# Decode attention: the first softmax ahead of a key turn, five value steps ahead of the second group's scores, and wq loaded in two parts

## Chip, cores, metric

One core of a Trainium2 chip. The metric is device time in microseconds (us), median over executions. Before the change: 326.44 us over three runs when the prediction was made (325.81 to 326.68). Repeats on one chip spread by 0.3 to 2%, and chips differ a little. A program on one core has no second die to compare with. In some groups 1 to 3 runs are marked slow, because they lie over 1.5% above the fastest run of the same kernel; the ratios leave these out, the medians include them.

## The reference

Two transformer layers that share weights and caches, one token for each of four sequences ("batches" below):

```python
x = x + attn(layernorm(x))     # wq, K and V caches, softmax, wo
x = x + ffn(layernorm(x))      # gelu(x@w_gate) * (x@w_up) @ w_down
x = x + attn(layernorm(x))     # the same weights, the same caches
x = x + ffn(layernorm(x))
# B=4, D=512, Hq=32, Hkv=8, Sk=4096, Dh=128, F=1792, bfloat16
```

The caches are 32 MB of keys and 32 MB of values. The kernel reads the keys once (they stay in SBUF for the second layer) and the values nearly twice.

## The kernel before

For each batch, 8 key heads are handled as two groups of 4. A key head is two tiles of 16 x 128; each tile is turned on VectorE (DVE) with a 32 x 32 block transpose, in place: a "key turn", 16 per batch. TensorE multiplies turned keys with queries into one PSUM bank per group (`scores`), DVE and ScalarE do the softmax, and TensorE multiplies the probabilities with the values in 16 "value steps" per batch, one step for each 0.5 MB unit. Values stream through a ring of 7 such slots. A load is issued from the SyncE queue as soon as the program order and a free slot allow.

The order of everything is the order of the program text; no scheduler moves anything. The part that the change touches, for one batch:

```python
        sc1 = new_scores(0)
        scores(sc1, ga, 0)
        turn(1 if first else GH)          # key turns 1 to 8 end here
        if two:
            vals2.step(...)               # second layer of the batch before
        scores(sc1, ga, 1)
        turn()                            # turn 9, a key of the second group
        p0 = soft(sc1)                    # max, exp ... of the first group
        turn()                            # 10
        ...
        soft_turn(p0)
        pe, den = soft_swap(p0, p1p), soft_den(p0)
        turn()                            # 11
        prob1[ga] = (pe, soft_recip(den))
        ...
        build_q1(b1, gb)
        turn()                            # 12
        vals.step(2)                      # value steps 1 and 2
        turn(3)                           # 13 to 15
        sc1 = new_scores(0)
        scores(sc1, gb, 0)                # needs turns 9, 11, 13 and 15
        turn()                            # 16
        vals.step(3)                      # 3 to 5
        scores(sc1, gb, 1)
        ...
        p0 = soft(sc1)
        vals.step(3)                      # 6 to 8
        ...
        vals.step(3)                      # 9 ..., need the second group's softmax
```

A value step, cut to what matters. After steps 4, 8 and 12 a copy on DVE takes two heads' sums out of PSUM (after steps 14 and 16 one head's); it is called the OT copy below:

```python
        def step(self, count=1):
            for _ in range(min(count, VB - self.n)):
                ...
                self.n += 1
                load_v()
                v = slot(held[b, g, s, t])
                for i in range(CH):
                    nc.tensor.matmul(self.ot[:, s % 2], lhsT=v[:, i, :], rhs=pe[:, s, c, :], ...)
                release(held.pop((b, g, s, t)))      # the slot is free
                load_v()                             # issue what now fits
                if self.n % (m * NT) == 0:           # m * NT is 4 (2 in the last four steps)
                    nc.vector.tensor_tensor(out=self.dst(...), in0=self.ot[...],
                                            in1=rden[...], op=ALU.mult)     # the OT copy
```

Of the kernel before, what the change touches and what calls it, by code (L numbers as in the profile page):

```python
# [9 lines left out]
BF16 = mybir.dt.bfloat16  # L10
# [5 lines left out]
P = 128  # L16
# [3 lines left out]
QD = 4  # L20
QS = P // QD
# [9 lines left out]
def kernel(  # L31
# [15 lines left out]
    _, Hkv, Sk, Dh = A_k_cache.shape  # L47
    HqDh = A_wq.shape[1]
    Hq = HqDh // Dh
    rep = Hq // Hkv  # L50
    F = B_w_gate.shape[1]
    assert Sq == 1 and Dh == P and rep == QD and Hkv % GH == 0
    KD = D // P
# [4 lines left out]
    NG = Hkv // GH  # L58
    HG = GH * rep
    NK = GH * BE  # L60
    W = 4 * QD
    TG = GH * NT
# [3 lines left out]
    wts = ctx.enter_context(tc.tile_pool(name="wts", bufs=1))  # L66
# [15 lines left out]

    dq = nc.sync

    wq_sb = wts.tile([P, KD, HqDh], BF16, name="wq_sb")
    wo_sb = wts.tile([P, Hq, D], BF16, name="wo_sb")
    wg_sb = wts.tile([P, KD, F], BF16, name="wg_sb")
    wu_sb = wts.tile([P, KD, F], BF16, name="wu_sb")
# [3 lines left out]
    wq_dram = A_wq.rearrange("(k p) n -> p k n", p=P)  # L92
# [22 lines left out]
    def groups(b):  # L115
        return [b % NG, (b + 1) % NG]
# [1 line left out]
    def cache_tile(cache, b, kvh, t, n=1):  # L118
        return cache[b, kvh].rearrange("(p c) d -> p c d", p=P)[:, t * CH:(t + n) * CH]

    def load_wq():
        dq.dma_start(out=wq_sb[:], in_=wq_dram)

    def load_rest():
        n = Hq // 4
# [84 lines left out]
    def new_rows():  # L210
        turn_row[0] += 1
        return ROWS[turn_row[0] % 2]
# [5 lines left out]
    def q_rows(b0, nb, g):  # L218
        bs = slice(b0, b0 + nb)
        rows = new_rows()  # L220
        for k in range(KD):
            for j in range(QD):
                n0 = (g * QD + j) * rep * Dh
                w = wq_sb[:, k, n0:n0 + rep * Dh].rearrange("p (m i e) -> p m e i", i=QS, e=2)
                nc.tensor.matmul(rows[j * QS:j * QS + nb, :], lhsT=xn_bf[:, k, bs], rhs=w,  # L225
                                 start=(k == 0), stop=(k == KD - 1))
        return rows
# [16 lines left out]
    def q_build(qm, g):  # L244
        qe = ps_sm.tile([P, NK, rep], FP32, name="qe", tag="sm")
        nc.tensor.matmul(qe[:], lhsT=t32_bf.rearrange("p a i -> p (a i)"),  # L246
                         rhs=qm.rearrange("p g n h -> p (g n) h"), start=True, stop=True)
        dst = qb[:, W:].rearrange("p (n x a h) -> p n x a h", x=2, a=QD, h=rep)[:, :, 0]
        nc.vector.tensor_tensor(  # L249
            out=dst,  # L250
            in0=qe[:].unsqueeze(2).broadcast_to([P, NK, QD, rep]),
            in1=amask[:].unsqueeze(1).unsqueeze(3).broadcast_to([P, NK, QD, rep]),
            op=ALU.mult)
# [98 lines left out]
    class Keys:  # L352
# [19 lines left out]
        def turn(self, count=1):  # L372
            for _ in range(count):
                kvh, t = self.tile(self.nt)
                self.nt += 1
                words = KT[kvh][t].rearrange("p c d -> p (c d)").bitcast(FP32)
                nc.vector.transpose(out=words, in_=words)  # L377

    def new_scores(bank):
        return ps_sc.tile([P, CH, QS], FP32, name="sc", tag=f"sc{bank}")  # L380

    def scores(sc, g, t):
        for be in range(BE):
            for s in range(GH):
                n = s * BE + be
                w0 = n * 2 * W + (W if t == 0 else 0)
                kt = KT[g * GH + s][t].rearrange("p c (b j e) -> p c b j e", b=NB, e=2)
                nc.tensor.matmul(sc[s * QS:(s + 1) * QS], lhsT=qb[:, w0:w0 + 2 * W],  # L388
                                 rhs=kt[:, :, be // 2, :, be % 2],
                                 start=(t == 0 and be == 0), stop=(t == NT - 1 and be == BE - 1))  # L390
# [22 lines left out]
    def soft_turn(p0):  # L413
        flat = p0[0].rearrange("p c j -> p (c j)")
        nc.vector.transpose(out=flat, in_=flat)  # L415

    def soft_den(p0):
        zx = p0[1]
        den = ps_sm.tile([P, GH, rep], FP32, name="den", tag="sm")
        nc.tensor.matmul(den[:], lhsT=mean_f[:, :], rhs=zx[:], start=True, stop=True)  # L420
        return den
# [26 lines left out]
    for b in range(B - 1):  # L448
        n = early[b]
# [72 lines left out]
    def attend(b2, b1, next_q=None, rest=None):  # L522
        two, first = b2 is not None, b1 == 0
        prob1, prob2 = {}, {}
        ga, gb = groups(b1)
        keys = Keys(b1)
        turn = keys.turn
        vals = Values(b1, 0, prob1, lambda k, m: OT_bf[:, k * rep:(k + m) * rep])
        vals2 = None
        if two:  # L530
            vals2 = Values(b2, 1, prob2, lambda k, m: OT2_bf[:, k * rep:(k + m) * rep, b2])
            sc2 = [new_scores(i) for i in range(NG)]
            seen["hold"] = True
            scores(sc2[0], ga, 0)
            keys.load(GH)
            qm1 = next_q()
            scores(sc2[0], ga, 1)
            keys.load(GH)
            q_build(qm1, gb)
            rest(1)  # L540
            for t in range(NT):
                scores(sc2[1], gb, t)
            if early[b2] < TG:
                keys.load(TG)
                seen["hold"], seen["whole"] = False, True
                load_v()
            else:
                keys.load(GH)
            p0 = soft(sc2[0])
            rest(1)  # L550
            soft_turn(p0)
            pe0, den0 = soft_swap(p0, p2p), soft_den(p0)
            rest(VB)
            qm = q_spread(q1_bf[:, ga, :, b1], amask, ga)
            turn()
            prob2[ga] = (pe0, soft_recip(den0))
            q_build(qm, ga)
            turn(3)
            vals2.step(2 * NT)
            if early[b2] == TG:  # L560
                keys.load(GH)
                seen["hold"], seen["whole"] = False, True
                load_v()
        else:
            load_wq()
            keys.load(2 * TG)
            load_v()
            make_identity(nc, ident_bf[:])
            build_consts()
            xT_ps = ps_sm.tile([P, KD, B], BF16, name="xT_ps", tag="sm")  # L570
            for k in range(KD):
                nc.tensor.transpose(xT_ps[:, k, :], x_bf[:B, k * P:(k + 1) * P], ident_bf[:B, :B])
            nc.vector.tensor_copy(out=XX[:, 0].rearrange("p b k -> p k b"), in_=xT_ps[:])
            ln_square(0, B)
            rstd1 = ln_rstd(B, ln_center(0, B))
            q_first(q_rows(0, B, 0), 0, rstd1)
            build_q1(0, 0)
            turn(TG - 1)
        sc1 = new_scores(0)
        scores(sc1, ga, 0)  # L580
        turn(1 if first else GH)
        if two:
            vals2.step(max(early[b2] - vals2.n - 1, 0))
        scores(sc1, ga, 1)
        turn()
        p0 = soft(sc1)
        turn()
        if two:
            vals2.step(early[b2] - vals2.n)
        soft_turn(p0)  # L590
        pe, den = soft_swap(p0, p1p), soft_den(p0)
        turn()
        prob1[ga] = (pe, soft_recip(den))
        if first:
            q_first(q_rows(0, B, 1), 1, rstd1)
        build_q1(b1, gb)
        turn()
        vals.step(2)
        turn(3)
        sc1 = new_scores(0)  # L600
        scores(sc1, gb, 0)
        turn()
        vals.step(3)
        scores(sc1, gb, 1)
        rows = new_rows()
        hp = 2 * rep
        heads = pairs(vals.order)
        p0 = soft(sc1)
        vals.step(3)
        soft_turn(p0)  # L610
        if not first:
            for i in range(2):
                out_proj(rows, OT_bf, heads[i], hp, i == 0)
        pe, den = soft_swap(p0, p1p), soft_den(p0)
        if two:
            p1 = soft(sc2[1])
        prob1[gb] = (pe, soft_recip(den))
        vals.step(3)
        if two:
            soft_turn(p1)  # L620
            pe1, den1 = soft_swap(p1, p2p), soft_den(p1)
            prob2[gb] = (pe1, soft_recip(den1))
        if first:
            vals.step(5)
            load_rest()
            seen["upto"] = len(loads)
            load_v()
            for i in range(3):
                out_proj(rows, OT_bf, heads[i], hp, i == 0, i == 2)
            y = y_select(y_rows(rows, 1), 1)  # L630
            return (y, OT_bf, heads[3], hp), vals2
        vals.step(2)
        out_proj(rows, OT_bf, heads[2], hp)
        vals.step()
        out_proj(rows, OT_bf, heads[4], rep, False, True)
        yc = y_rows(rows, 1)
        vals.step()
        y = y_select(yc, 1)
        vals.step()
        return (y, OT_bf, heads[5], rep), vals2  # L640
# [64 lines left out]
    for b in range(B):  # L705
# [17 lines left out]
        def next_q():  # L723
            return q_spread(turn_rows(q_rows(b, 1, gb), 512)[:, :, 0], am, gb)
# [46 lines left out]
```

## Time and profile before

| | before |
|---|---|
| median | 326.44 us |
| profiled execution, span | 327.2 us |
| bytes from HBM | 113.5 MB |
| DMA engines busy with the kernel's queue | 89.6% |
| TensorE, VectorE, ScalarE busy | 65%, 52%, 9% |

The page of the kernel before: the mean busy share of the 16 DMA engines and the GB/s in 40 equal slices of 8.2 us, the chain of waits by engine, and the group of key turns (count, then busy us and mean ns of one, then idle time ahead of it).

```profile
DMA  7999959999939998899989977999999999999910
GB/s 275 430 420 422 412 207 398 346 377 383 345 106 363 422 423 361 314 365 417 366 307 351 425 290 253 400 372 393 381 411 424 420 400 381 352 374 408 414 40 3
...
DMA 40%; PE 28%; DVE 19%; SPq 8%; issue 3%; ACT 1%; DVEq 0%; ACTq 0%
...
L377 DVE STREAM_TRANSPOSE kt<-kt 128x1024 f32<-128x1024 f32 x64 | 75.0, 1216 | 5.1 <-DMA kt<-in_A_k_cache_dram 5.1
```

Where nothing stalls, the DMA engines move about 420 GB/s and 1 MB takes 2.5 us. The largest share of the chain is DMA. So this kernel loses time where the DMA row falls: slices 6, 12, 16, 17, 21, 24 and 25, and the end.

Finer, the stretches in which the first-layer attention of each batch lets the DMA engines run dry (columns: stretch, length, busy us of TensorE, its weight loads, VectorE, ScalarE, GpSimd, then granted TensorE clock, DMA share, GB/s). The last line is the same place in the fourth batch:

```profile
40.00:44.00 4.00, 1.58 (x13) 0.56 (x13) 4.00 (x4) 0.00 (x0) 0.00 (x0) 0.50 0.70 280
44.00:48.00 4.00, 4.00 (x73) 1.81 (x65) 0.24 (x2) 0.00 (x0) 0.00 (x0) 0.50 0.34 101
...
128.00:132.00 4.00, 3.71 (x69) 2.10 (x72) 1.53 (x3) 0.00 (x0) 0.00 (x0) 0.50 0.69 219
...
192.00:196.00 4.00, 1.87 (x14) 0.56 (x13) 3.79 (x4) 0.00 (x0) 0.00 (x0) 0.50 0.65 266
196.00:200.00 4.00, 4.00 (x79) 2.10 (x75) 0.34 (x2) 0.00 (x0) 0.00 (x0) 0.50 0.44 145
...
272.00:276.00 4.00, 2.52 (x44) 1.05 (x42) 1.10 (x4) 0.00 (x0) 0.00 (x0) 0.50 0.99 406
```

In the first three batches the ring is full there, and value steps 3 to 5, which would free slots, stand in TensorE's queue behind the second group's scores, which wait for key turns. In the fourth batch there is no such hole (0.99).

The same place in the fourth batch in order of time on VectorE (start, length, engine, line, operation; in brackets the idle time before it and what ended it). The line at 254.60 is key turns 12 to 16:

```profile
248.10 1.25 DVE L377 STREAM_TRANSPOSE kt<-kt 128x1024 f32<-128x1024 f32 x1 [1.03 <-DMA kt<-in_A_k_cache_dram]
249.27 0.65 DVE L394 TENSOR_REDUCE m<-sc 128x1 f32<-128x512 f32 x1
...
254.60 5.74 DVE L377 STREAM_TRANSPOSE kt<-kt 128x1024 f32<-128x1024 f32 x5
262.12 0.17 DVE L513 TENSOR_TENSOR OT_bf<-ot,rden 128x8 bf16<-128x8 f32 x1 [1.78 <-PE ot L505]
264.38 0.69 DVE L394 TENSOR_REDUCE m<-sc 128x1 f32<-128x512 f32 x1 [2.10 <-PE sc L388]
```

And on TensorE:

```profile
254.04 0.58 PE L505 MATMUL ot<-pe,ring 128*128 128x4 bf16 x16
256.87 0.59 PE L505 MATMUL ot<-pe,ring 128*128 128x4 bf16 x16 [2.24 <-DMA ring<-in_A_v_cache_dram]
...
259.27 1.87 PE L388 MATMUL sc<-kt,qb 128*32 128x512 bf16 x13 [1.27 <-DVE kt L377]
261.07 1.44 PE L505 MATMUL ot<-pe,ring 128*128 128x4 bf16 x48
```

Step 1 runs at 254.04 without a wait, step 2 at 256.87 after waiting for a value load, the second group's scores follow their turns, and steps 3 to 5 come at 261.07 without any wait.

### The profile page before, as it was taken

What the parts mean: (1) busy time and instruction counts of PE and PEld (TensorE: products, weight loads), DVE (VectorE), ACT (ScalarE), POOL (GpSimd) and SP (SyncE); (2) the same over time, 40 slices, a digit from 0 to 9 for tenths busy, and PEclk for the clock granted to TensorE, in tenths of its full rate; (3) what the DMA queues carried; (4) which work ended last, traced back from release to release, by engine and by line L of the source; (5) the groups of instructions that cost most, each with busy time, mean ns of one, the idle gap of its engine ahead of it and who ended that gap; (6) DMA issues with size and microseconds to landing.
All of it is one profiled execution on the core that took longest, in us unless ns stands there. A gap on an engine that the chain in (4) does not pass through costs nothing.

```text
span 327.2 us, 8603 instructions
## 1 busy us (share of the span) xinstructions
PE 211.0 (65%) x3844; PEld 121.5 (37%) x3844; DVE 170.9 (52%) x481; ACT 29.1 (9%) x70; POOL 0.7 (0%) x6
## 2 busy tenths in 40 slices
PE   1224575243676346978876359799874597998875
PEld 0001344121323122555433125456331265654655
DVE  5097752013348657525457884254498752545133
ACT  0002002000002020300020102100101030002200
POOL 0000000000000000000000000000000000000000
PEclk9999555555558555555595555556765555559555
DMA  7999959999939998899989977999999999999910
GB/s 275 430 420 422 412 207 398 346 377 383 345 106 363 422 423 361 314 365 417 366 307 351 425 290 253 400 372 393 381 411 424 420 400 381 352 374 408 414 40 3
DMA packets 26789, 114.07 MB, mean 349 GB/s; under 512 B 2296, under 2 KB 8192, under 8 KB 18944
## 3 DMA queue, kind: packets, MB, share of 16 engines
q1 hardware_dynamic: 26752, 113.53, 89.6%
q8 instruction: 30, 0.49, 0.6%
q14 instruction: 7, 0.06, 0.0%
HBM read 113.51 MB, written 0.00 MB: 347 GB/s over the span
## 4 chain that ended last, share of the span: by engine, by line
DMA 40%; PE 28%; DVE 19%; SPq 8%; issue 3%; ACT 1%; DVEq 0%; ACTq 0%
DMA kt<-in_A_k_cache_dram 20%; DMA ring<-in_A_v_cache_dram 17%; PE sc L388 8%; DVE kt L377 7%; PE ot L505 7%; PE rows L314 3%; DMA wd_sb<-in_B_w_down_dram 3%; SPq L127 3%; SPq L133 3%; PE y L347 2%; DVE rows L215 2%; PE rows L280 2%; PE rows L225 2%; PE x L434 1%; DVE pp L415 1%
## 5 line engine op out<-in xcount | busy, mean ns | idle before, releaser
L388 PE MATMUL sc<-kt,qb 128*32 128x512 bf16 x512 | 63.7, 547 | 26.6 <-DVE kt L377 22.4
L505 PEld LDWEIGHTS <-ring 128*128 128x128 bf16 x1920 | 59.5, 105 | 51.3 <-DMA ring<-in_A_v_cache_dram 28.3
L377 DVE STREAM_TRANSPOSE kt<-kt 128x1024 f32<-128x1024 f32 x64 | 75.0, 1216 | 5.1 <-DMA kt<-in_A_k_cache_dram 5.1
L505 PE MATMUL ot<-pe,ring 128*128 128x4 bf16 x1920 | 62.1, 166 | 21.8 <-DMA ring<-in_A_v_cache_dram 20.7
L215 DVE STREAM_TRANSPOSE rows<-rows 128x512 f32<-128x512 f32 (+1 forms) x23 | 16.2, 706 | 43.6 <-PE rows L225 24.7
L388 PEld LDWEIGHTS <-qb 128*32 128x32 bf16 x512 | 17.5, 116 | 56.6 <-issue 35.9
L407 ACT ACTIVATE pp<-sc,nm 128x512 bf16<-128x512 f32 x16 | 11.0, 687 | 163.7 <-DVE junk L403 163.7
L513 DVE TENSOR_TENSOR OT_bf<-ot,rden 128x8 bf16<-128x8 f32 (+1 forms) x40 | 6.5, 164 | 35.7 <-PE ot L505 35.2
L225 PE MATMUL rows<-wq_sb,xn_bf 128*1 128x512 bf16 (+1 forms) x160 | 18.7, 615 | 9.6 <-DMA wq_sb<-in_A_wq_dram 9.3
L434 PE MATMUL x<-pp,ident_bf 128*32 128x128 bf16 x256 | 9.0, 282 | 20.5 <-DVE pp L415 20.4
L280 PE MATMUL rows<-wo_sb,OT_bf 128*1 128x512 bf16 (+1 forms) x136 | 17.2, 611 | 7.7 <-DMA wo_sb<-in_A_wo_dram 6.7
L394 DVE TENSOR_REDUCE m<-sc 128x1 f32<-128x512 f32 x16 | 10.8, 672 | 14.6 <-PE sc L388 14.6
L434 PEld LDWEIGHTS <-ident_bf 128*32 128x32 bf16 x256 | 6.5, 118 | 26.1 <-issue 24.5
L415 DVE STREAM_TRANSPOSE pp<-pp 128x512 bf16<-128x512 bf16 x16 | 11.3, 704 | 7.7 <-ACT pp L407 7.7
L225 PEld LDWEIGHTS <-xn_bf 128*1 128x1 bf16 (+1 forms) x160 | 4.6, 110 | 17.7 <-issue 16.4
L437 ACT CAST pe<-x 128x512 bf16<-128x512 f32 x16 | 9.4, 585 | 20.1 <-PE x L434 20.1
L347 PE MATMUL y<-H_bf,wd_sb 128*128 128x1 bf16 (+1 forms) x280 | 8.5, 165 | 2.8 <-DVE H_bf L340 1.7
L249 DVE TENSOR_TENSOR qb<-qe,amask 128x256 bf16<-128x256 f32 x16 | 6.8, 424 | 5.7 <-PE qe L246 5.7
L347 PEld LDWEIGHTS <-wd_sb 128*128 128x128 bf16 x280 | 8.0, 103 | 4.1 <-DMA wd_sb<-in_B_w_down_dram 3.0
L246 PE MATMUL qe<-qm,t_bf 128*128 128x64 bf16 x16 | 3.4, 214 | 9.1 <-DVE qm L236 7.0
L420 PE MATMUL den<-zx,mean_f 128*128 128x16 f32 x32 | 8.9, 357 | 0.0
L425 DVE RECIPROCAL rden<-den 128x16 f32<-128x16 f32 x16 | 4.0, 250 | 9.1 <-PE den L420 8.6
(78 smaller groups left out, 124.5 us busy)
## 6 DMA issues: line engine op xcount, KB each, us to landing
ring<-in_A_v_cache_dram SPq DMA_DIRECT2D x37, 1024.0 KB, 8.3
ring<-in_A_v_cache_dram SPq DMA_DIRECT2D x44, 512.0 KB, 7.0
kt<-in_A_k_cache_dram SPq DMA_DIRECT2D x20, 1024.0 KB, 15.7
kt<-in_A_k_cache_dram SPq DMA_DIRECT2D x24, 512.0 KB, 8.3
wq_sb<-in_A_wq_dram SPq DMA_DIRECT2D x1, 4096.0 KB, 12.6
wo_sb<-in_A_wo_dram SPq DMA_DIRECT2D x4, 1024.0 KB, 12.2
kt<-in_A_v_cache_dram SPq DMA_DIRECT2D x8, 512.0 KB, 9.1
wg_sb<-in_B_w_gate_dram SPq DMA_DIRECT2D x1, 1792.0 KB, 13.5
```

What stands on the lines that cost most here:

```text
L127: dq.dma_start(out=wo_sb[:, i * n:(i + 1) * n], in_=wo_dram[:, i * n:(i + 1) * n])
L215: nc.vector.transpose(out=rows[:, :n], in_=rows[:, :n])
L225: nc.tensor.matmul(rows[j * QS:j * QS + nb, :], lhsT=xn_bf[:, k, bs], rhs=w, start=(k == 0), stop=(k == KD - 1))
L280: nc.tensor.matmul(rows[r0:r0 + lhsT.shape[-1], :], lhsT=lhsT, rhs=wo_sb[:, i, :], start=(start and n < QD), stop=(stop and n >= hp - QD))
L347: nc.tensor.matmul(y[:, k], lhsT=wd_sb[:, c, k * P:(k + 1) * P], rhs=H_bf[:, c, :], start=(c == 0 and k == 0), stop=(c == KF - 1), skip_gr ...
L377: nc.vector.transpose(out=words, in_=words)
L388: nc.tensor.matmul(sc[s * QS:(s + 1) * QS], lhsT=qb[:, w0:w0 + 2 * W], rhs=kt[:, :, be // 2, :, be % 2], start=(t == 0 and be == 0), stop= ...
L394: nc.vector.tensor_reduce(out=m[:], in_=sc.rearrange("p c j -> p (c j)"), axis=AX.X, op=ALU.max)
L407: nc.scalar.activation(out=pp[:], in_=sc[:], func=ACT.Exp, bias=nm[:, 0:1], scale=scale, accum_out=ls[:])
L415: nc.vector.transpose(out=flat, in_=flat)
L434: nc.tensor.matmul(x[a * QS:(a + 1) * QS, s], lhsT=ident_bf[:, s * QS:(s + 1) * QS], rhs=pT[:, a], start=True, stop=True, skip_group_check ...
L505: nc.tensor.matmul(self.ot[:, s % 2], lhsT=v[:, i, :], rhs=pe[:, s, c, :], start=(c == 0), stop=(c == C - 1), skip_group_check=True)
```

## The change

Its intent: free ring slots earlier and so fill the DMA holes (five value steps ahead of the second group's scores), start the first group's softmax earlier (ahead of turn 9), and let the first batch begin on half of wq.

```diff
-    wq_sb = wts.tile([P, KD, HqDh], BF16, name="wq_sb")
+    wq_sb = [wts.tile([P, KD, HG * Dh], BF16, name=f"wq_sb{g}") for g in range(NG)]
...
-    def load_wq():
-        dq.dma_start(out=wq_sb[:], in_=wq_dram)
+    def load_wq(g):
+        n = HG * Dh
+        dq.dma_start(out=wq_sb[g][:], in_=wq_dram[:, :, g * n:(g + 1) * n])
...
-            load_wq()
-            keys.load(2 * TG)
+            load_wq(0)
+            keys.load(TG)
+            load_wq(1)
+            keys.load(TG)
...
         scores(sc1, ga, 1)
-        turn()
         p0 = soft(sc1)
         turn()
...
         build_q1(b1, gb)
         turn()
-        vals.step(2)
-        turn(3)
+        vals.step(5)
+        turn(4)
         sc1 = new_scores(0)
         scores(sc1, gb, 0)
         turn()
-        vals.step(3)
+        vals.step(1)
         scores(sc1, gb, 1)
...
         p0 = soft(sc1)
-        vals.step(3)
+        vals.step(2)
         soft_turn(p0)
```

More of the change, by code (lines that the diff above doesn't have):

```diff
@@ L222, in q_rows @@
             for j in range(QD):
-                n0 = (g * QD + j) * rep * Dh
-                w = wq_sb[:, k, n0:n0 + rep * Dh].rearrange("p (m i e) -> p m e i", i=QS, e=2)
+                n0 = j * rep * Dh
+                w = wq_sb[g][:, k, n0:n0 + rep * Dh].rearrange("p (m i e) -> p m e i", i=QS, e=2)
                 nc.tensor.matmul(rows[j * QS:j * QS + nb, :], lhsT=xn_bf[:, k, bs], rhs=w,
```

## The prediction

> **What bounds it now.** The page: DMA engines 90% busy, mean 349 GB/s, 420 where nothing stalls; the chain of waits is 40% DMA, nearly all keys and value ring. Time is lost where the DMA engines run dry. By stretches of 4 us they do so in each first-layer attention but the last, because the 7-slot value ring is full: 40 to 48 us (about 3.9 us idle), 128 to 140 (2.0), 188 to 200 (4.1), 256 to 268 (none). Another 6 us (88 to 96) and the tail after 312 belong to the dense chain, which the change does not touch. The attackable sum is 10 us, 3%.
>
> **What the change does.** No work is added; one DMA issue more.
> 1. Value steps 3 to 5 go before the second group's scores, so three ring slots come free 3 to 7 us earlier (third batch: the load that step 3 releases was issued at 197.1, and could be at 190.5). This fills the gaps named.
> 2. The softmax goes before one key turn (1.2 us): 0.5 us gained in batches 3 and 4; in batch 2 it waits for a value landing (115.7), so nothing.
> 3. The first wq half lets the first group start 5 us earlier; but the second group's keys still land last at 33.6 and values at 36.1, 39.9, 42.5.
>
> **The cost I see.** The copy of OT after step 4 now stands on DVE ahead of key turns 12 to 16 (the built order shows it), and DVE takes its queue in order (the Trainium skill, "PSUM — Partial Sum Buffer", calls the VectorE queue strict FIFO). Step 4 needs value units that land at 39.9, 126.9, 192.3 and 256.8. Five turns of 1.15 us then follow, where before they filled that very wait (from 39.5, 124.8, 190.0, 254.7). I reckon the second group's scores end later by about 1.9, 3.5, 2.0 and 2.0 us, and with them step 9, which releases the next loads. So the DMA hole moves to before step 9: an idle queue needs 2.3 us from issue to data (issued 45.42, landed 50.23, of which 2.5 is transfer; the skill's "DMA: Bandwidth & Descriptors" gives a fixed cost of about 2.0; the trace's number is used).
>
> Landing of the load that step 9 releases (estimates from the trace's landings):
> - batch 1: 59.0 to 59.8 (+0.8)
> - batch 2: 144.8 to 146.7 (+1.8)
> - batch 3: 212.2 to 211.5 (-0.6)
> - batch 4: 276.2 to 276.4 (+0.2)
>
> Each batch's rest is tied to these landings, so they add: +2.2 us. As such a reordering is usually made to gain, I take +1.6.
>
> **Prediction: 328.0 us, 8 in 10 between 324.0 and 331.0. Faster by over 2%: 0.04; within 2%: 0.92; slower by over 2%: 0.04.**
>
> **What would show it.** DMA share of 40 to 46, 128 to 134 and 192 to 198 rises to about 1.0; new holes of 1 to 3 us near 50 to 57, 139 to 144, 204 to 209. DVE idles 2 to 4 us before the OT copy ahead of the turns, released by PE ot. First softmax max near 24 us instead of 29.06, without effect at 59. Second-group score max at about 50, 137, 201.7, 266 instead of 48.1, 133.4, 199.8, 264.3. DMA bytes and busy times unchanged.
>
> **What would make it wrong.** If values land before step 4 asks, the turns are not held and up to 2 us a batch is won (320 to 322). If the earlier loads don't count, 2 us a batch is lost (334). If the first batch's head start reaches the weights, 1 to 3 us comes off.

## The result

The change makes the kernel slower: 338.06 us (337.19 to 339.0, four runs) against 326.52 us (four runs), ratio 1.0358 with a 95% interval of 1.032 to 1.0396. A ratio here and below is the mean time of one kernel's fast runs over the mean of the other's fast runs of the same rounds, so it is not quite the ratio of the two medians that are quoted.

The page of the changed kernel, the same lines:

```profile
DMA  7999976999759999589989994899999967999920
GB/s 273 423 416 419 412 302 239 351 379 379 304 136 420 419 421 386 218 321 380 366 296 414 421 382 170 318 403 399 370 424 418 416 213 269 410 373 379 413 82 2
...
DMA 46%; PE 25%; DVE 16%; SPq 8%; issue 2%; ACT 2%; DVEq 0%
...
L378 DVE STREAM_TRANSPOSE kt<-kt 128x1024 f32<-128x1024 f32 x64 | 75.4, 1218 | 3.4 <-DMA kt<-in_A_k_cache_dram 3.4
```

Busy time per turn and the bytes are as before; the DMA mean falls to 338 GB/s, and the DMA share of the chain rises from 40% to 46%. Line numbers are one higher (key turns L378, scores L389, value steps L506, OT copy L514).

The stretches again:

```profile
40.00:44.00 4.00, 2.49 (x51) 1.64 (x52) 2.95 (x4) 0.00 (x0) 0.00 (x0) 0.50 1.03 418
44.00:48.00 4.00, 2.33 (x29) 0.87 (x28) 2.87 (x3) 0.00 (x0) 0.00 (x0) 0.50 1.00 414
48.00:52.00 4.00, 2.96 (x55) 1.58 (x53) 1.36 (x6) 0.46 (x1) 0.00 (x0) 0.50 0.20 41
...
136.00:140.00 4.00, 4.00 (x73) 1.99 (x72) 1.20 (x4) 0.00 (x0) 0.00 (x0) 0.50 0.53 188
140.00:144.00 4.00, 3.50 (x70) 2.19 (x63) 2.46 (x11) 2.64 (x7) 0.00 (x0) 0.50 0.41 141
...
192.00:196.00 4.00, 1.78 (x59) 1.63 (x58) 1.92 (x4) 0.16 (x1) 0.00 (x0) 0.50 1.01 393
196.00:200.00 4.00, 1.56 (x32) 0.97 (x30) 3.62 (x5) 0.00 (x0) 0.00 (x0) 0.50 1.05 420
...
208.00:212.00 4.00, 3.40 (x87) 2.73 (x83) 2.51 (x8) 1.72 (x5) 0.00 (x0) 0.50 0.29 84
...
272.00:276.00 4.00, 3.85 (x77) 1.97 (x80) 1.36 (x6) 0.08 (x1) 0.00 (x0) 0.76 0.33 78
```

The old holes are filled as intended: 40 to 48 went from 0.70 and 0.34 to 1.03 and 1.00, and 192 to 200 from 0.65 and 0.44 to 1.01 and 1.05. New and deeper ones stand a little later: 48 to 52 at 0.20, 136 to 144 at 0.53 and 0.41, 208 to 212 at 0.29, and 272 to 276, where there was none, at 0.33.

VectorE in the fourth batch, which begins 4.84 us later than before (its first key load is issued at 234.40 instead of 229.56):

```profile
254.08 0.69 DVE L395 TENSOR_REDUCE m<-sc 128x1 f32<-128x512 f32 x1 [1.95 <-PE sc L389]
...
255.38 1.24 DVE L378 STREAM_TRANSPOSE kt<-kt 128x1024 f32<-128x1024 f32 x1
...
259.45 1.23 DVE L378 STREAM_TRANSPOSE kt<-kt 128x1024 f32<-128x1024 f32 x1
265.65 0.17 DVE L514 TENSOR_TENSOR OT_bf<-ot,rden 128x8 bf16<-128x8 f32 x1 [4.97 <-PE ot L506]
265.73 5.74 DVE L378 STREAM_TRANSPOSE kt<-kt 128x1024 f32<-128x1024 f32 x5
274.44 0.69 DVE L395 TENSOR_REDUCE m<-sc 128x1 f32<-128x512 f32 x1 [2.96 <-PE sc L389]
```

Turn 11 is at 259.45. Then VectorE is idle for 4.97 us, though the last of the batch's keys landed at 260.80, until the OT copy at the head of its queue gets its sums from TensorE, and only then do the five turns run (265.73 to 271.47). The second group's score max starts at 274.44, which is 40.04 us after the batch's first key load, against 34.82 (264.38 less 229.56) before. TensorE shows what the OT copy waits for:

```profile
258.89 0.58 PE L506 MATMUL ot<-pe,ring 128*128 128x4 bf16 x16
262.11 0.59 PE L506 MATMUL ot<-pe,ring 128*128 128x4 bf16 x16 [2.63 <-DMA ring<-in_A_v_cache_dram]
264.60 1.01 PE L506 MATMUL ot<-pe,ring 128*128 128x4 bf16 x32 [1.91 <-DMA ring<-in_A_v_cache_dram]
267.09 0.59 PE L506 MATMUL ot<-pe,ring 128*128 128x4 bf16 x16 [1.48 <-DMA ring<-in_A_v_cache_dram]
267.61 1.12 PE L389 MATMUL sc<-kt,qb 128*32 128x512 bf16 x3
270.40 1.87 PE L389 MATMUL sc<-kt,qb 128*32 128x512 bf16 x13 [1.67 <-DVE kt L378]
```

Step 2 waits for its value load until 262.11, steps 3 and 4 for theirs until 264.60, step 5 until 267.09; the scores then wait for the turns until 270.40.

The same account for all batches, from the issue of each batch's first key load (in the last row from the first value load that goes into key tiles, which only the last layer has). The repeat is the unedited changed kernel, on another chip; its growth, too, is against the one profile of the kernel before, so differences between chips are in it:

| part | before, us | changed | growth | repeat, growth | predicted |
|---|---|---|---|---|---|
| start to second batch's keys | 93.85 | 95.38 | +1.5 | +1.7 | +0.8 |
| to third batch's keys | 69.83 | 72.11 | +2.3 | +1.2 | +1.8 |
| to fourth batch's keys | 65.88 | 66.91 | +1.0 | -0.1 | -0.6 |
| to last layer's values | 64.30 | 69.50 | +5.2 | +5.4 | +0.2 |
| rest | 33.3 | 33.2 | -0.1 | +0.7 | 0 |

The four batches were predicted to add 2.2 us and added 10.0 in the profiled run. Half of it comes from the fourth.

### The profile page after: what moved, and what is told of

Read it like the earlier page. It is cut to its first block, busy times and chain, and to the rows that moved or that the text cites. A ratio compares the mean times of both kernels' runs of the same rounds, so it can differ in the third digit from the quotient of the medians.

```text
span 337.1 us, 8603 instructions
## 1 busy us (share of the span) xinstructions
PE 209.5 (62%) x3844; PEld 121.4 (36%) x3844; DVE 171.1 (51%) x481; ACT 29.1 (9%) x70; POOL 0.7 (0%) x6
## 4 chain that ended last, share of the span: by engine, by line
DMA 46%; PE 25%; DVE 16%; SPq 8%; issue 2%; ACT 2%; DVEq 0%
DMA ring<-in_A_v_cache_dram 30%; DMA kt<-in_A_k_cache_dram 13%; PE sc L389 8%; PE ot L506 6%; DVE kt L378 5%; DMA wd_sb<-in_B_w_down_dram 3%; SPq L134 3%; SPq L128 3%; PE rows L315 2%; PE y L348 2%; PE rows L226 2%; DVE pp L416 2%; ACT pp L408 1%; PE x L435 1%; DVE rows L216 1%
## 5 line engine op out<-in xcount | busy, mean ns | idle before, releaser
L506 PE MATMUL ot<-pe,ring 128*128 128x4 bf16 x1920 | 62.8, 166 | 35.5 <-DMA ring<-in_A_v_cache_dram 34.6
L506 PEld LDWEIGHTS <-ring 128*128 128x128 bf16 x1920 | 59.9, 105 | 65.1 <-DMA ring<-in_A_v_cache_dram 42.1
L389 PE MATMUL sc<-kt,qb 128*32 128x512 bf16 x512 | 62.0, 535 | 25.1 <-DVE kt L378 22.0
L378 DVE STREAM_TRANSPOSE kt<-kt 128x1024 f32<-128x1024 f32 x64 | 75.4, 1218 | 3.4 <-DMA kt<-in_A_k_cache_dram 3.4
L389 PEld LDWEIGHTS <-qb 128*32 128x32 bf16 x512 | 17.2, 114 | 53.6 <-issue 30.4
L514 DVE TENSOR_TENSOR OT_bf<-ot,rden 128x8 bf16<-128x8 f32 (+1 forms) x40 | 6.5, 163 | 41.9 <-PE ot L506 41.4
L281 PE MATMUL rows<-wo_sb,OT_bf 128*1 128x512 bf16 (+1 forms) x136 | 16.5, 582 | 8.5 <-DMA wo_sb<-in_A_wo_dram 7.3
L226 PE MATMUL rows<-wq_sb,xn_bf 128*1 128x512 bf16 (+1 forms) x160 | 18.0, 595 | 4.6 <-DMA wq_sb<-in_A_wq_dram 4.3
L315 PE MATMUL rows<-wu_sb,xn_bf 128*1 128x448 bf16 x64 | 6.7, 567 | 2.9 <-DMA wu_sb<-in_B_w_up_dram 2.9
```

What stands on the lines that cost most here:

```text
L226: nc.tensor.matmul(rows[j * QS:j * QS + nb, :], lhsT=xn_bf[:, k, bs], rhs=w, start=(k == 0), stop=(k == KD - 1))
L281: nc.tensor.matmul(rows[r0:r0 + lhsT.shape[-1], :], lhsT=lhsT, rhs=wo_sb[:, i, :], start=(start and n < QD), stop=(stop and n >= hp - QD))
L315: nc.tensor.matmul(rows[j * QS:j * QS + nb, :KF * QS], lhsT=xn_bf[:, k, bs], rhs=w[:, j], start=(k == 0), stop=(k == KD - 1))
L378: nc.vector.transpose(out=words, in_=words)
L389: nc.tensor.matmul(sc[s * QS:(s + 1) * QS], lhsT=qb[:, w0:w0 + 2 * W], rhs=kt[:, :, be // 2, :, be % 2], start=(t == 0 and be == 0), stop= ...
```

## Experiments

Fourteen runs, all correct; `e12_after_again` is the changed kernel once more. The three parts of the change are named throughout: steps (5, 1, 2 instead of 2, 3, 3), softmax (ahead of turn 9), halves (wq in two loads). "Before" in the table is the median of the kernel before on the same chip; e1 to e4 ran on one chip, e5 to e8 on a second, e9 to e14 on a third (in two sittings).

| run | edit | median | before | ratio (95%) |
|---|---|---|---|---|
| e1_turns_first | all three; steps 4, 5 after the turns | 326.12 | 327.95 | 0.996 (0.991 to 1.001) |
| e2_steps_back | softmax + halves | 327.34 | 327.95 | 0.999 (0.995 to 1.002) |
| e3_steps_alone | steps | 330.96 | 327.95 | 1.012 (1.005 to 1.018) |
| e4_three_steps | softmax + halves, steps 3, 3, 2 | 325.49 | 327.95 | 0.991 (0.986 to 0.995) |
| e5_steps_and_wq | steps + halves | 331.35 | 328.52 | 1.010 (1.005 to 1.016) |
| e6_steps_and_softmax | steps + softmax | 335.16 | 328.52 | 1.024 (1.017 to 1.031) |
| e7_softmax_alone | softmax | 331.64 | 328.52 | 1.013 (1.007 to 1.018) |
| e8_wq_alone | halves | 326.54 | 328.52 | 0.992 (0.985 to 0.998) |
| e9_two_turns_first | all three; two turns before steps 4, 5 | 327.97 | 328.48 | 1.002 (0.995 to 1.009) |
| e10_three_steps_and_wq | halves, steps 3, 3, 2 | 323.86 | 328.48 | 0.991 (0.985 to 0.997) |
| e11_turns_first_softmax_back | steps + halves; steps 4, 5 after the turns | 326.15 | 328.48 | 0.997 (0.992 to 1.003) |
| e12_after_again | the change | 337.71 | 328.48 | 1.030 (1.022 to 1.038) |
| e13_last_batch_only | halves; the rest in batch 4 alone | 330.64 | 326.36 | 1.013 (1.008 to 1.017) |
| e14_all_but_last_batch | halves; the rest in batches 1 to 3 | 332.02 | 326.36 | 1.019 (1.015 to 1.023) |

### Is it the OT copy on VectorE?

The theory: the copy holds the turns back, they hold the scores, these hold step 9 and the loads behind it. Rival A: TensorE takes its steps in order, so steps 3 to 5, waiting for values, hold the scores whatever VectorE does. Rival B: the softmax or the halves did it.

`e1_turns_first`, an edit of the changed kernel. TensorE's order and the DMA queue's are identical to those of the changed kernel (compared in the built programs, and the two traces agree); only the place of the OT copy on VectorE differs.

```diff
-        vals.step(5)
-        turn(4)
+        vals.step(3)
+        turn(4)
+        vals.step(2)
```

> The changed kernel with steps 4 and 5 called after the turns instead of before: on DVE the four turns 12 to 15 stand ahead of the OT copy of step 4 again; TensorE's and the DMA queue's orders are those of the changed kernel. Theory (the OT copy on DVE holds the turns back): most of the loss goes; second-group score max near 47.3, 134.5, 199.5, 266.5 in the before kernel's time frame, total 320 to 325 us. Rival A (TensorE's own queue: steps 3 to 5 wait for values and hold the scores, whatever DVE does): stays at 336 to 339. Rival B (the loss comes from the softmax or the wq halves): stays at 336 to 339.

Measured: 0.996. All of the loss goes with the place of one short copy among the turns. The median, 326.12, is a little above the 320 to 325 that were expected, on a chip where the kernel before took 327.95. In the time frame of before, the second group's score maxes came at 47.05, 133.5, 198.2 and 266.1, 0.3 to 1.3 us sooner than expected. VectorE in the fourth batch (its keys are first loaded at 223.52):

```profile
248.34 5.74 DVE L378 STREAM_TRANSPOSE kt<-kt 128x1024 f32<-128x1024 f32 x5
254.01 0.13 DVE L514 TENSOR_TENSOR OT_bf<-ot,rden 128x8 bf16<-128x8 f32 x1
254.06 1.22 DVE L378 STREAM_TRANSPOSE kt<-kt 128x1024 f32<-128x1024 f32 x1
260.08 0.69 DVE L395 TENSOR_REDUCE m<-sc 128x1 f32<-128x512 f32 x1 [4.79 <-PE sc L389]
```

The five turns (11 to 15) run in one piece, the copy finds its sums ready, turn 16 follows. The score max is 36.56 us after the first key load: 3.48 us sooner than in the changed kernel, but still 1.74 later than before. TensorE tells why:

```profile
252.76 1.01 PE L506 MATMUL ot<-pe,ring 128*128 128x4 bf16 x32 [1.91 <-DMA ring<-in_A_v_cache_dram]
255.27 0.58 PE L506 MATMUL ot<-pe,ring 128*128 128x4 bf16 x16 [1.49 <-DMA ring<-in_A_v_cache_dram]
255.78 1.90 PE L389 MATMUL sc<-kt,qb 128*32 128x512 bf16 x16
```

All turns that the first scores need were done at 254.08; the scores began at 255.78, after step 5, which had waited for a value load. That is rival A at work. So of the 5.2 us by which this score max came later in the changed kernel, 3.5 are the copy on VectorE and 1.7 the value steps in TensorE's own queue. The batch as a whole does not keep the 1.7: in e1 it takes 65.05 us, 0.75 more than before, against 5.2 more in the changed kernel.

`e9_two_turns_first` gives the dose between:

```diff
-        vals.step(5)
-        turn(4)
+        vals.step(3)
+        turn(2)
+        vals.step(2)
+        turn(2)
```

> The changed kernel with two of the four turns ahead of steps 4 and 5 and so ahead of the OT copy; orders on TensorE and the DMA queue unchanged. With none ahead the ratio was 1.036, with all four 0.996. Theory (each turn behind the copy is paid with its 1.15 us, less what a full DMA queue hides): in between, 1.005 to 1.025; last turn of each batch ends 2.3 us sooner after the OT copy than in the changed kernel. Rival (only the first turn behind the copy counts, or something else that moving all four happened to mend): at one of the ends.

Measured: 1.002, with 1.030 for the unedited change on the same chip. The size is a little under the expected band: the first two turns that get out from behind the copy are worth 2.8%, the last two (to e1's 0.996) 0.6%, within the intervals perhaps nothing. The fourth batch shows it: the score max comes 36.59 us after the first key load with two turns ahead and 36.56 with four. Past two turns TensorE's wait for step 5 is the later of the two, and more turns don't help. The last turn ends 3.58 us after the OT copy's start instead of 5.82, the 2.3 us that were expected.

### Which part of the change costs what?

`e2_steps_back`, an edit of the changed kernel, and `e3_steps_alone`, an edit of the kernel before:

```diff
 # e2                                # the changed kernel
-        vals.step(5)
+        vals.step(2)
         turn(4)
...
-        vals.step(1)
+        vals.step(3)
         scores(sc1, gb, 1)
...
-        vals.step(2)
+        vals.step(3)
         soft_turn(p0)
```

```diff
 # e3                                # the kernel before
-        vals.step(2)
+        vals.step(5)
         turn(3)
...
-        vals.step(3)
+        vals.step(1)
         scores(sc1, gb, 1)
...
-        vals.step(3)
+        vals.step(2)
         soft_turn(p0)
```

> The changed kernel with the value steps of the kernel before (2, 3, 3) and the other two parts left in. Theory: without the OT copy ahead of the turns the loss is gone, and the first batch's head start (turns done by 40 instead of 44) now counts, 3 to 4 us; total 321 to 325. Rival B (softmax ahead of the turn, or wq halves, cost the time): 333 to 339.

> The kernel before with only the value steps changed (5, 1, 2). Only four turns (13 to 16) stand behind the OT copy instead of five, so 1.15 us less is lost in each batch. Theory: 332 to 336. Rival B: 320 to 327, as the steps would be harmless or good.

Measured: 0.999 and 1.012. With the steps back the loss is gone, and the steps cost by themselves, but both sizes missed. e2 was expected to win 3 to 7 us from the head start and won 0.5. The head start itself is there (the second batch's keys are asked for at 90.95 instead of 93.85); in the profiles the later parts give 0.8 us of it back, and the rest of the miss stays open. e3 cost less than expected, and 1.012 and 0.999 don't multiply to 1.036. So the remaining combinations were run.

`e5_steps_and_wq`, an edit of the changed kernel, and `e6_steps_and_softmax`, an edit of e3:

```diff
 # e5                                # the changed kernel
         scores(sc1, ga, 1)
+        turn()
         p0 = soft(sc1)
...
         vals.step(5)
-        turn(4)
+        turn(3)
```

```diff
 # e6                                # e3
         scores(sc1, ga, 1)
-        turn()
         p0 = soft(sc1)
...
         vals.step(5)
-        turn(3)
+        turn(4)
```

> The kernel before with the value steps 5, 1, 2 and the wq halves; the softmax stays behind its key turn, so four turns stand behind the OT copy. The steps alone cost 1.2 per cent and the whole change 3.6, so two parts act together; which two is open. Theory (the softmax's move puts a fifth turn behind the OT copy): as the steps alone, ratio 1.005 to 1.017. Rival (the wq halves act with the steps): 1.028 to 1.04.

> The kernel before with the value steps 5, 1, 2 and the softmax ahead of its turn, wq in one load; five turns stand behind the OT copy. Theory: as the whole change, ratio 1.03 to 1.04. Rival (wq halves act with the steps): 1.01 to 1.02.

Measured: 1.010 and 1.024. e5 is as expected; e6 falls between the theory's band and the rival's, with an interval (1.017 to 1.031) that reaches into the first. The halves give nothing that can be seen once the steps are moved (1.012 without, 1.010 with, on different chips). That fits the prediction's reason: the first batch's steps then wait for a value load, which lands at 39.95 us before and after the change. The softmax does cost with the steps. 1.024 is about what 1.012 and 1.013 (next) give as a product, so the ratios need no joint action of the two. The profiles leave it possible: the fourth batch grew by 2.1 us with the steps alone, by 1.7 with the softmax alone and by 5.3 with both (one execution each, the last being the slowest of e6's four). The whole change is 1.036 on one chip and 1.030 on another; whether it is more than e6's 1.024 can't be told from these intervals.

`e7_softmax_alone` and `e8_wq_alone`, edits of the kernel before:

```diff
 # e7
         scores(sc1, ga, 1)
-        turn()
         p0 = soft(sc1)
...
         vals.step(2)
-        turn(3)
+        turn(4)
```

```diff
 # e8, with the rest of the halves' edits from the change
-            load_wq()
-            keys.load(2 * TG)
+            load_wq(0)
+            keys.load(TG)
+            load_wq(1)
+            keys.load(TG)
```

> The kernel before with the softmax ahead of its turn alone. Theory: 0.5 us won in the third and fourth batches, up to 1.15 us lost in the second, where the turn that was done while DVE idled at 112 is now done after the softmax; ratio 0.997 to 1.004. If the softmax's move by itself cost what is missing, it would be 1.01 or more.

> The kernel before with wq in two halves alone. The first batch's turns are done 3 to 4 us sooner, so step 9 and the weights behind it come sooner: first key load of the second batch near 91 instead of 93.9 and ratio 0.988 to 0.996. If the halves cost anything, over 1.0.

Measured: e8 0.992, within the expected ratio, though the head start is smaller than expected: the first batch's turns end at 42.82 instead of 44.07, and the second batch's keys come at 92.28 instead of 93.85, not near 91. e7 1.013, against an expected 0.997 to 1.004: a plain miss. VectorE in the first batch, first the kernel before, then e7:

```profile
25.58 2.33 DVE L377 STREAM_TRANSPOSE kt<-kt 128x1024 f32<-128x1024 f32 x2
29.06 0.69 DVE L394 TENSOR_REDUCE m<-sc 128x1 f32<-128x512 f32 x1 [1.15 <-PE sc L388]
...
38.33 5.74 DVE L377 STREAM_TRANSPOSE kt<-kt 128x1024 f32<-128x1024 f32 x5
```

```profile
25.37 1.20 DVE L377 STREAM_TRANSPOSE kt<-kt 128x1024 f32<-128x1024 f32 x1
29.10 0.69 DVE L394 TENSOR_REDUCE m<-sc 128x1 f32<-128x512 f32 x1 [2.53 <-PE sc L388]
...
38.37 6.86 DVE L377 STREAM_TRANSPOSE kt<-kt 128x1024 f32<-128x1024 f32 x6
```

Before, two turns ran ahead of the score max, in time that VectorE would have spent waiting for the scores (1.15 us of it remained). In e7 one ran, VectorE waited 2.53 us, and the max began at the same time (29.10 against 29.06). The turn that was left behind is the sixth of the row at 38.37, which ends at 45.23 instead of 44.07. So the softmax gained nothing here and paid a turn. In the third batch its max did come 0.57 us sooner after the first key load, as predicted, in the fourth only 0.07; but the turn left behind costs more, and the second group's score max came 1.15, 1.15, 0.59 and 1.09 us later in the four batches. Over the kernel the five parts grew by 1.4, 0.4, 0.4, 1.7 and 0.3 us.

### The fourth batch

The prediction had put 0.2 us on it and the profiles show 5.2. Both kernels have the halves; in batches that are not "changed", the softmax and the steps are those of the kernel before:

```diff
+        changed = b1 == B - 1                # e13; e14: b1 < B - 1
         scores(sc1, ga, 1)
+        turn(0 if changed else 1)
         p0 = soft(sc1)
...
-        vals.step(5)
-        turn(4)
+        vals.step(5 if changed else 2)
+        turn(4 if changed else 3)
... (1 if changed else 3, then 2 if changed else 3)
```

> The wq halves everywhere, the softmax's move and the 5, 1, 2 steps in the fourth batch alone. The halves alone stood at 0.992. If the fourth batch costs 4.5 to 5.5 us: 1.003 to 1.011. If it costs the 0.2 us that the prediction put on it: 0.988 to 0.997.

> The whole change in all batches but the fourth, which keeps the old order. The whole change stood at 1.030 to 1.036. If the fourth batch costs 4.5 to 5.5 us: 1.012 to 1.022. If it costs 0.2 us: 1.028 to 1.036.

Measured: 1.013 and 1.019. e13's 1.013 is a little over its expected band, e14 is within its own. e13 less the halves' 0.992 (on another chip) is 2.1%, or 6.8 us; e14 is 1.1 to 1.7% under the whole change, or 3.6 to 5.5 us. Each of these differences has an uncertainty of about 2 to 3 us. In the profiles the fourth batch takes 68.34 us in e13 and 63.03 us in e14, against 64.30 before and 69.50 changed. So the fourth batch alone is worth about 5 us, in edits of that batch as in the profiles.

### A better order

`e4_three_steps`: three steps ahead, so that slots come free but no OT copy is due before the turns.

```diff
-        vals.step(5)
+        vals.step(3)
         turn(4)
...
-        vals.step(1)
+        vals.step(3)
         scores(sc1, gb, 1)
```

> The changed kernel with three steps ahead of the second group's scores instead of five (3, 3, 2): the third step releases its ring slots early, and no OT copy falls due ahead of the turns. Theory: 319 to 325, and the load that step 3 releases goes out as early as in the changed kernel. Rival A: TensorE still waits for step 3's values ahead of the scores; 326 to 332.

`e10_three_steps_and_wq` is e4 and `e11_turns_first_softmax_back` is e1, each with the softmax back; `e12_after_again` is the changed kernel unedited.

```diff
 # e10 from e4, e11 from e1
         scores(sc1, ga, 1)
+        turn()
         p0 = soft(sc1)
...
         vals.step(3)
-        turn(4)
+        turn(3)
```

> The changed kernel with three steps ahead and the softmax back behind its turn, so that turn 9 is done while DVE waits for the scores. Softmax alone cost 1.3 per cent, three steps with the two other parts stood at 0.991. Theory: 0.975 to 0.988. If the softmax's cost belongs to the kernel before alone, 0.989 to 0.995.

> The changed kernel with steps 4 and 5 called after the turns and the softmax back behind its turn. Theory: 0.978 to 0.990, from 0.996 less the softmax's 1.3 per cent. If the softmax's cost belongs to the kernel before alone, 0.992 to 0.999.

> The changed kernel unedited, on the chip of the other runs of this call, as a mark for them: 1.032 to 1.040. If it comes to 1.02 to 1.03, as the steps with the softmax did on another chip, then the wq halves added nothing to the loss and the difference was the chip's.

Measured: e4 0.991, e10 0.991, e11 0.997, e12 1.030. e4's median is half a us over the band. e12's ratio is just below its band, at the edge of the rival reading that the halves add nothing; its interval (1.022 to 1.038) allows both. Putting the softmax back, which was expected to give another 1%, gave nothing: 0.991 stays 0.991, and 0.996 becomes 0.997. For e1 a trace suggests why: in its fourth batch the scores started 1.70 us after the turns they need, so one more turn behind the softmax is free there. For e4 this doesn't hold in every batch: in its third the scores still wait for the turns, and the second group's score max comes 0.9 us later after the first key load than in e10, while in the first batch it comes 0.8 sooner. Why the two come out equal is not shown. e10 and e4 beat both kernels by a little, 0.9% under the kernel before; e8's halves alone (0.992) do as well within the intervals, so it is not shown that three early steps add anything to the halves.

## Why the prediction was wrong

It said 328.0 us, 324.0 to 331.0, with 92% for "within 2%"; the kernel took 338.06, 3.6% more than before.

**What held.** The mechanism was the one named: the OT copy ahead of turns 12 to 16, VectorE idle before it (6.19, 3.15, 2.06 and 4.97 us in the four batches, where 2 to 4 were forecast), the old holes filled and new ones just before step 9. The Trainium skill's "PSUM — Partial Sum Buffer", section "Engine vs sequencer instructions", calls VectorE's queue strict FIFO, and this trace agrees: turns whose keys had landed stood behind a 0.17 us copy. e1 shows that undoing that order alone takes the loss away. In the first three batches the sizes were near as well. With the later start of each batch taken off, the second group's score max came at 50.06, 137.2 and 201.6, predicted "about 50, 137, 201.7". The load that step 9 releases landed at 59.88 in the first batch (predicted 59.8), and with the later start off at 146.9 and 211.4 in the second and third (146.7, 211.5). The idle-queue time of 2.3 us held too: the load issued at 50.56 landed at 55.38, which less 2.5 of transfer is 2.3.

**The step that failed: "Step 4 needs value units that land at 39.9, 126.9, 192.3 and 256.8".** The last of these is wrong. The load that lands at 256.8 is the one that step 2 waits for: TensorE's step at 256.87 is a single one and is the second, and in the changed kernel steps 3 and 4 wait together for the next load (264.60, or 259.8 in the time frame of before). That next load is 1 MB, so about 2.5 us later. With 259.3 in place of 256.8, the prediction's own sum gives a score max of 269.4 (copy at 260.3, four turns to 265.1, then 1.9 of scores, 0.5 of step 6, 1.9 of scores). Measured was 269.6; the prediction had 266. The pattern of the other batches had been carried over without a look at which step each landing ended.

**The same batch, second term: "batch 4: 276.2 to 276.4 (+0.2)".** It took most of the delay of step 9 to be hidden by a full DMA queue. But the delay was 5.2 us rather than 2.0, and nothing was left in the queue: the DMA share of 272 to 276 is 0.33. The trace has no landing for this load in the changed kernel, but the step that needs it ran without a wait at 284.56, or 279.7 in the time frame of before, so it was up to 3.5 us later. The load behind it, which step 11 releases, took 8.5 us from issue to the step that waited for it in both kernels. On the chain that ended last, before and changed:

```profile
270.20 8.50 DMA ring<-in_A_v_cache_dram
```

```profile
280.24 8.49 DMA ring<-in_A_v_cache_dram
```

So the delay went through in full, +5.2 us. e13 and e14 agree with the size. Why this load took as long with an emptier queue is not shown.

**The softmax term: "0.5 us gained in batches 3 and 4; in batch 2 ... nothing".** Alone, it costs 1.3%. The gain itself was there in the third batch (0.57 us) and all but absent in the fourth (0.07). In the first batch the turn was done in a VectorE wait and cost nothing there. Left behind, it put the second group's score max 0.59 to 1.15 us later in every batch. I had counted the turn among the five behind the copy, but not that it costs without the copy too.

**"Each batch's rest is tied to these landings, so they add".** Nearly. The first batch's load landed 0.9 us late and the batch ended 1.5 us late (1.7 in the repeat); in the third the load landed 0.8 us early and the batch ended 1.0 us late in one profile and 0.1 early in the other. So what follows these landings adds up to a microsecond or so. Instruction fetches stand at other places of the two traces, but no run here isolates that.

**"As such a reordering is usually made to gain, I take +1.6".** This moved the centre from the worked-out sum towards a hope. It was small beside the rest, but nothing in the trace stood behind it. The warning "if the earlier loads don't count, 2 us a batch is lost (334)" was the nearest to what happened and got too little weight.

What stays open: whether the halves make the whole change worse than steps and softmax together (1.030 and 1.036 against 1.024, on different chips), and the rest of the first batch's and third batch's growth.

## What to carry to other kernels

When work is moved forward on one engine, look for the small consumer that moves with it onto another engine's in-order queue, and ask what is now standing behind it; here a 0.17 us copy held five 1.15 us turns. When slots are freed earlier in a loop, ask for every iteration which wait ends last there, and settle which load each wait belongs to by counting the steps in the trace, since one iteration that differs can be half of the result. A piece of work that runs in a wait is free where it is, and moving something ahead of it gains only if that something was not waiting too.

## What the Trainium skill lacked or had wrong

- "Runtime: NRT & Kernel Launch", section "Instruction fetch mechanics": it says that instructions come in 16 KiB blocks through a DMA queue of the sequencer's own and that the cost of crossing a block is mostly hidden. The blocks are in this trace (30 of them, 0.49 MB), and each held a DMA engine for 0.9 to 1.4 us. Where the DMA engines are the limit they may not be hidden: the value load that landed after the block fetched at 37.6 us came 3.85 us behind the one before it (36.10 to 39.95), where 1 MB takes 2.5 us otherwise. That the fetch is the cause was not isolated, and two other loads speak against a rule: with blocks fetched at 126.94 and 262.97 us, the 1 MB loads under way landed 2.50 us behind the ones before them.
- "DMA: Bandwidth & Descriptors", section "Anatomy of one DMA — SWDGE (gpsimd) path": a fixed cost of about 2.0 us and then bytes at 436 GB/s, for the other issuing path. For loads issued from SyncE the page gives no time from issue to landing. Here an idle queue took 2.3 us (50.56 to 55.38 us for 1 MB, of which 2.5 us is transfer at 420 GB/s).
- No page that I found says that a copy out of PSUM, emitted with the matmuls that fill it, takes a place in VectorE's order, so that moving the matmuls earlier moves a block there. Measured: 1.036 with the copy ahead of five turns, 0.996 with the copy behind four of them and all else equal.
